# Grouping 1024 tokens in a fused attention and soft-MoE kernel, with the slot sums in the next group's burst of logits

## The chip, the cores and the metric

The kernel runs on one core of a Trainium2 chip. The time is device microseconds of one execution of the whole program; three runs of the kernel before took 1529.78, 1530.56 and 1531.02 us. A profiled execution is one further run, with every instruction's start and length recorded.

In the profile the engines are: PE, TensorE's matrix products; PEld, its weight loads; DVE, VectorE; ACT, ScalarE; POOL, GpSimd; SP, SyncE, which issues the DMAs here.

## What is computed

Two stages, all in f32. The first is an attention without softmax, for 8 batches of 2496 tokens, with keys and queries both z (64 wide) and values v (256 wide):

```
scores = z @ z.T / 2496
x      = u * (max(scores, 0)**2 @ v)            # 8 x 2496 x 256
```

The second is a soft mixture of experts on the 19968 tokens x, with 32 slots (8 experts of 4 slots):

```
logits     = x @ phi                            # 19968 x 32
d          = exp(logits - logits.max(0))        # over all tokens
slot_input = (d / d.sum(0)).T @ x               # 32 x 256: the slot sums
slot_out   = relu(slot_input @ w1) @ w2         # per expert
c          = exp(logits - logits.max(1)); c /= c.sum(1)     # combine weights
out        = c @ slot_out
```

## The kernel before, in words

The attention goes chunk by chunk: a chunk is up to 512 queries of one batch (512, 512, 512, 512, 448; the last batch is cut so that it ends with two chunks of 256). Each chunk has 5 steps over the keys, each step 4 key tiles of 128, and each step two halves. `scores` (line 175) makes two score tiles on PE (tile `sc`), ScalarE applies relu and square (tile `r`), and VectorE splits the result into a rounded part `ph` and its remainder `pl`. `attend` (line 216) then multiplies these with the values, split in the same way, into the tile `acc`: 24 products in a half step, on two row halves of 64 at a time, so that two products run side by side. The main loop (line 465) lets `scores` run one step ahead: in front of each half of `attend` it calls `between`, which runs the functions left in the list `begin`, then at most one piece of `work`, then `pair`, which makes the scores of the next step. Lists `middle` and `behind` hold work that other engines do between relu and square, and behind the remainders.

PE, ScalarE and VectorE are wrapped in `InOrder` (line 38): their instructions keep the order in which the code issues them. All of them therefore have line 46 in the profile, the line of the wrapper, and are told apart by their tiles. DMAs on SP have no such wrapper.

When a chunk is complete, `finish_chunk` (line 276) multiplies `acc` with `u` into the tile `xg` of a group of 512 tokens, 39 groups in all. A complete group puts four calls of the generator `group` (line 291) into `work`, and they run in the half steps of the next chunk, from the second step on:

1. logits (tile `lg`): 16 products of the 32-slot phi with 128 tokens each, laid out so that token quarter t stands on rows 32 t to 32 t + 31 of the result. Each row half (h) of the 128 feature rows gives its own partial result in its own half `ps[:, h]` of the tile, 512 columns each; VectorE adds the two into L, takes the maximum and updates the running maximum. ScalarE's exponentials E wait in `middle`.
2. transposes of the tokens (tile `tr`), which ScalarE copies to `xt`. Columns 256 and 257 of `xt` hold ones.
3. transposes of L and E (tile `le`). From L's transpose the combine weights `cw` follow, through `begin` and `middle`.
4. slot sums (tile `sl`): 8 products of E's transpose with `xt`, 258 columns wide; column 256 is thereby the sum of the exponentials. VectorE rescales `slot_acc` by the change of the maximum, adds half 0, and then half 1.

All four tiles share one buffer of the pool `ms_ps`. The accumulators `acc` (2), the score tiles (2) and this tile fill the PSUM memory. Behind the attention part come the transposes of `cw` (`turn`, line 392), the experts and the output; line numbers from 500 on belong to them. There ScalarE and VectorE each copy one half of the columns of a tile `sT_ps` (lines 528 and 529).

Of the kernel before, what the change touches and what calls it, by code (L numbers as in the profile page):

```python
# [20 lines left out]
NW = 32  # L21
KT = 20
QC = 512
NQ = 5
NG = N // 512
SMALL, LARGE = [(0, 2), (37, 2), (34, 3)], [(g, 4) for g in range(2, 34, 4)]
ROT = S - QC * (NQ - 1)
NP = KT // 4
# [21 lines left out]
def attn_soft_moe_kernel(ctx, tc, uT, v, zz, phi, ww, outT):  # L50
    nc = tc.nc

    pe, act, dve = (InOrder(tc, x) for x in (nc.tensor, nc.scalar, nc.vector))

    cpool = ctx.enter_context(tc.tile_pool(name="cpool", bufs=1))
# [4 lines left out]
    ms_ps = att_ps.enter_context(tc.tile_pool(name="ms_ps", bufs=1, space=PSUM))  # L60
# [3 lines left out]
    xpool = moe.enter_context(tc.tile_pool(name="xpool", bufs=1))  # L64
    HALF = [slice(0, 64), slice(64, 128)]
# [49 lines left out]
    xt = [xpool.tile([P, 4, 258], F32, name=f"xt{i}") for i in range(2)]  # L115
    slot_acc = [cpool.tile([P, 258], F32, name=f"slot_acc{i}") for i in range(2)]
    runmax = [cpool.tile([P, 1], F32, name=f"runmax{i}") for i in range(2)]
    cw = cpool.tile([P, NG, P], F32, name="cw")

    def constants():  # L120
        make_identity(nc, ident)


        nc.gpsimd.memset(esel, 0.0)
        nc.gpsimd.memset(rsel, 0.0)
        for h in range(4):
            rows = slice(h * NS, (h + 1) * NS)
            nc.gpsimd.tensor_copy(
                esel[rows, :, 0:SE], ident[rows, rows].rearrange("k (e s) -> k e s", s=SE)
            )  # L130
# [8 lines left out]
        for t in xt:  # L139
            nc.gpsimd.memset(t[:, :, 256:258], 1.0)  # L140
# [135 lines left out]
    def finish_chunk(b, ch, acc):  # L276
        _, _, n, t0 = ch
        ut = ut_.pop(t0)
        s = 0
        while s < n:  # L280
            g, o = divmod(t0 + s, 512)
            w = min(n - s, 512 - o)
            if g not in xg_:
                xg_[g] = wk.tile([P, 2, 512], F32, tag="xg", name=f"xg_{g}")
            dve.tensor_mul(xg_[g][:, :, o : o + w], acc[:, :, s : s + w], ut[:, :, s : s + w])
# [5 lines left out]
    def group(g):  # L291

        x = xg_.pop(g)

        ps = ms_ps.tile([P, 2, 512], F32, tag="ms", name=f"lg_{g}")
# [7 lines left out]
        L = wk.tile([P, P], F32, tag="L", name=f"L_{g}")  # L305
        E = wk.tile([P, P], F32, tag="E", name=f"E_{g}")
        m = wk.tile([P, 4], F32, tag="m", name=f"m_{g}")
        mnew, mold = runmax[g % 2], runmax[(g + 1) % 2]
        dve.tensor_copy(L, ps[:, 0, 0:P])
        dve.tensor_add(L, L, ps[:, 1, 0:P])  # L310
        if g == 0:
            dve.reduce_max(mnew, L, axis=AX.X)
        else:
            dve.reduce_max(m[:, 0:1], L, axis=AX.X)
            dve.tensor_max(mnew, m[:, 0:1], mold)
            dve.tensor_sub(m[:, 2:3], mold, mnew)
        dve.tensor_scalar_mul(m[:, 1:2], mnew, -1.0)

        def exps():
            act.activation(E, L, AF.Exp, bias=m[:, 1:2])  # L320
            if g:
                act.activation(m[:, 3:4], m[:, 2:3], AF.Exp)

        middle.append(exps)
        yield

        ps = ms_ps.tile([P, 2, 512], F32, tag="ms", name=f"tr_{g}")
        for t in range(4):
            for c in range(2):
                for h, rows in enumerate(HALF):  # L330
                    pe.transpose(
                        ps[:, h, t * P + c * 64 : t * P + (c + 1) * 64],
                        x[rows, c, t * P : (t + 1) * P], ident[rows, rows],
                    )
        xs = xt[g % 2]
        act.copy(
            xs[:, :, 0:D].rearrange("p t (h q) -> p h t q", h=2),
            ps.rearrange("p h (t q) -> p h t q", q=P),
        )
        yield  # L340

        ps = ms_ps.tile([P, 2, 512], F32, tag="ms", name=f"le_{g}")
        for k, m_ in enumerate((L, E)):
            for h, rows in enumerate(HALF):
                pe.transpose(ps[:, h, k * 64 : (k + 1) * 64], m_[rows], ident[rows, rows])
        le = wk.tile([P, 2, P], F32, tag="le", name=f"le_{g}")
        act.copy(le, ps[:, :, 0:P])
        rm = wk.tile([P, 2, 4], F32, tag="rm", name=f"rm_{g}")
        lt = le[:, :, 0:64].rearrange("p h (b s) -> p h b s", s=NS)
        cg = cw[:, g].rearrange("p (h b s) -> p h b s", b=2, s=NS)  # L350

        def rows_of(i):
            return rm[:, i].rearrange("p (h b) -> p h b", b=2)

        def spread(i):
            return rows_of(i).unsqueeze(3).to_broadcast([P, 2, 2, NS])

        def combine():
            dve.tensor_reduce(rows_of(0), lt, axis=AX.X, op=ALU.max)
            dve.tensor_sub(cg, lt, spread(0))  # L360
            middle.append(combine_exp)

        def combine_exp():
            act.activation(cw[:, g], cw[:, g], AF.Exp)
            begin.append(combine_sum)

        def combine_sum():
            dve.tensor_reduce(rows_of(1), cg, axis=AX.X, op=ALU.add)
            dve.tensor_scalar_add(rm[:, 1], rm[:, 1], 1e-9)
            dve.reciprocal(rm[:, 1], rm[:, 1])  # L370
            dve.tensor_mul(cg, cg, spread(1))

        begin.append(combine)
        yield

        ps = ms_ps.tile([P, 2, 512], F32, tag="ms", name=f"sl_{g}")
        for t in range(4):
            e = le[:, t // 2, 64 + t % 2 * NS : 64 + (t % 2 + 1) * NS]
            for h, rows in enumerate(HALF):
                pe.matmul(  # L380
                    ps[t * NS : (t + 1) * NS, h, 0:258], e[rows], xs[rows, t], start=True, stop=True
                )
        snew, sold = slot_acc[g % 2], slot_acc[(g + 1) % 2]
        if g == 0:
            dve.tensor_copy(snew, ps[:, 0, 0:258])
        else:
            dve.scalar_tensor_tensor(
                snew, sold, m[:, 3:4], ps[:, 0, 0:258], op0=ALU.mult, op1=ALU.add
            )
        dve.tensor_add(snew, snew, ps[:, 1, 0:258])  # L390

    def turn(g0, ng):

# [103 lines left out]


    ep = ctx.enter_context(tc.tile_pool(name="ep", bufs=1))
    sfin = slot_acc[(NG - 1) % 2]  # L500

    mfin = runmax[(NG - 1) % 2]
# [27 lines left out]
    for eg in range(2):  # L532
        nc.tensor.matmul(
            pn[:, eg : eg + 1], fsel[:, eg * P : (eg + 1) * P],
            sfin[:, 256:257], start=True, stop=True,
        )
    rs = ep.tile([P, 2], F32, name="rs")
    nc.vector.tensor_scalar_add(rs, pn[:, 0:2], 1e-9)
# [165 lines left out]
```

## Time and profile before

| | before |
|---|---|
| median of 3 runs | 1530.56 us |
| the profiled execution's own time | 1529.76 us |
| its span, first to last instruction | 1528.0 us |
| mean granted TensorE clock | 0.985 |
| PE busy | 1499.4 us, 15332 products |
| VectorE busy | 1158.0 us |
| ScalarE busy | 1033.0 us |

Busy time of an engine is the union of its instructions' times. Products overlap on PE, and their ends are modelled, so that what a burst costs is read from the starts of the work behind it. In the chain of waits each row is a start, a length and the work that stood on the path to the end. The page's group rows give an operation, its tiles (out<-in), shapes and count, then busy time and mean ns of one, then the engine's idle time ahead of it and who ended it. In timeline rows a start, a length and a merged run of equal instructions are followed in brackets by the idle time ahead of them and its releaser.

### The profile page before, as it was taken

The page shows a single profiled execution, that of the slowest core. Times are in us where ns is not written, and L with a number is a line of the kernel's source. Part 1 is how long each engine was busy: PE and PEld are TensorE (multiplying, and loading weights), DVE is VectorE, ACT ScalarE, POOL GpSimd, SP SyncE. Part 2 cuts the span into 40 slices and gives each one's busy share as a digit, 9 for nine tenths or more (in the row PEclk, how much of TensorE's full clock was granted, in tenths as well). Part 3 has the DMA queues.
Part 4 walks back from the last instruction along what each step waited for, and adds up shares of the span by engine and source line. Part 5 has one row for each costly group of instructions (what it writes and reads, how often), then busy time and mean ns, then how long its engine had stood idle before and what let it go on. Part 6 is the DMA issues. An engine that isn't in the chain of part 4 may idle for free.

```text
span 1528.0 us, 38187 instructions
## 1 busy us (share of the span) xinstructions
PE 1499.4 (98%) x15332; PEld 1203.0 (79%) x15332; DVE 1158.0 (76%) x2466; ACT 1033.0 (68%) x2043; POOL 3.2 (0%) x23
## 2 busy tenths in 40 slices
PE   8999999999999999999999999999999999999985
PEld 6877887788777887778777787778877788778853
DVE  6878866877778876788778886788777887676753
ACT  7777766767667666777668676676667776666543
POOL 0000000000000000000000000000000000000000
PEclk9999999999999999999999999999999999999995
DMA  4111200111001210112001110011101131000659
GB/s 146 29 29 55 57 24 27 41 52 54 15 22 48 57 36 15 29 55 59 20 16 50 54 57 15 22 48 50 43 15 29 49 122 45 26 9 8 242 236 392
DMA packets 36657, 91.62 MB, mean 60 GB/s; under 512 B 3712, under 2 KB 6272, under 8 KB 34432
## 3 DMA queue, kind: packets, MB, share of 16 engines
q1 hardware_dynamic: 36480, 89.18, 18.2%
q8 instruction: 121, 1.98, 0.5%
q14 instruction: 56, 0.46, 0.1%
HBM read 68.71 MB, written 20.45 MB: 58 GB/s over the span
## 4 chain that ended last, share of the span: by engine, by line
PE 96%; DMA 2%; DVE 1%; ACT 0%; issue 0%; DVEq 0%; SPq 0%; ACTq 0%
PE acc L46 70%; PE sc L46 19%; DMA outT<-ot 2%; PE lg L46 2%; PE sl L46 2%; PE tr L46 1%; PE h L552 0%; PE po L574 0%; DVE ot L634 0%; PE le L46 0%; PE pf L628 0%; DMA zr<-in_zz 0%; PE cT L396 0%; DVE cw L397 0%; PE so L605 0%
## 5 line engine op out<-in xcount | busy, mean ns | idle before, releaser
L46 PE MATMUL acc<-ph,v 64*128 64x512 f32 (+2 forms) x6384 | 996.7, 383 | 0.0
L46 PEld LDWEIGHTS acc<-ph,v 64*128 64x128 f32 x6384 | 617.5, 185 | 120.2 <-issue 0.2
L46 ACT ACTIVATE r<-sc 128x512 f32<-128x512 f32 (+2 forms) x820 | 428.4, 575 | 388.3 <-PE sc L46 386.8
L46 PE MATMUL acc<-pl,v 64*128 64x512 f32 (+2 forms) x3190 | 639.4, 382 | 0.0
L46 DVE TENSOR_TENSOR pl<-r,ph 128x512 fp32r<-128x512 f32 (+4 forms) x819 | 546.0, 667 | 66.8 <-PE acc L46 1.4
L46 DVE CAST ph<-r 128x512 fp32r<-128x512 f32 (+2 forms) x820 | 336.1, 410 | 240.6 <-ACT r L46 237.6
L46 ACT ACTIVATE r<-r 128x512 f32<-128x512 f32 (+2 forms) x820 | 455.0, 610 | 0.0
L46 PEld LDWEIGHTS acc<-pl,v 64*128 64x128 f32 x3190 | 318.8, 185 | 57.5
L46 PE MATMUL sc<-z,z 64*128 64x512 f32 (+2 forms) x1920 | 275.8, 391 | 0.0
L46 PEld LDWEIGHTS sc<-z,z 64*128 64x128 f32 x1920 | 170.9, 185 | 46.0 <-issue 18.2
L46 PE MATMUL sc<-z 64*128 64x512 f32 (+2 forms) x480 | 69.9, 393 | 0.0
L46 DVE TENSOR_TENSOR z<-zr,z 64x512 fp32r<-64x512 f32 x80 | 54.9, 686 | 2.5
L46 DVE TENSOR_TENSOR v<-vr,v 128x512 fp32r<-128x512 f32 x80 | 54.9, 686 | 1.6 <-ACT v L46 1.4
L46 ACT CAST v<-vr 128x512 fp32r<-128x512 f32 x80 | 49.4, 618 | 8.9 <-PE sc L46 8.9
L46 PEld LDWEIGHTS sc<-z 64*128 64x128 f32 x480 | 43.1, 185 | 10.3 <-issue 4.9
L46 DVE TENSOR_TENSOR xg<-acc,ut 128x512 f32<-128x512 f32 (+7 forms) x71 | 49.7, 736 | 1.8 <-PE acc L46 1.8
L46 ACT CAST z<-zr 64x512 fp32r<-64x512 f32 x80 | 49.6, 620 | 1.9
L46 ACT COPY xt<-tr 128x1024 f32<-128x1024 f32 x39 | 39.5, 1013 | 11.7 <-PE tr L46 11.7
L634 DVE COPY ot<-pf 128x1024 f32<-128x1024 f32 (+2 forms) x22 | 24.3, 1102 | 21.2 <-DMA outT<-ot 16.3
L628 PE MATMUL pf<-cp,soh 32*128 32x512 f32 (+2 forms) x176 | 27.2, 587 | 10.7 <-ACT ot L634 8.4
L634 ACT COPY ot<-pf 128x1024 f32<-128x1024 f32 (+2 forms) x22 | 20.2, 917 | 25.2 <-DMA outT<-ot 19.8
L628 PEld LDWEIGHTS pf<-cp,soh 32*128 32x128 f32 x176 | 14.1, 258 | 22.9 <-ACT ot L634 16.5
(86 smaller groups left out, 481.3 us busy)
## 6 DMA issues: line engine op xcount, KB each, us to landing
vr<-in_v SPq DMA_DIRECT2D x80, 256.0 KB, 2.7
w<-in_w SPq DMA_DIRECT2D x32, 512.0 KB, 5.8
outT<-ot SPq DMA_DIRECT2D x16, 1024.0 KB, 8.4
ut<-in_uT SPq DMA_DIRECT2D x31, 512.0 KB, 3.7
zr<-in_zz SPq DMA_DIRECT2D x40, 256.0 KB, 2.7
ut<-in_uT SPq DMA_DIRECT2D x8, 448.0 KB, 3.4
outT<-ot SPq DMA_DIRECT2D x4, 512.0 KB, 5.4
outT<-ot SPq DMA_DIRECT2D x2, 768.0 KB, 5.7
```

What stands on the lines that cost most here:

```text
L46: return lambda *a, **k: self.tc.keep_in_program_order(f(*a, **k))
L628: nc.tensor.matmul(pf[t // 2][:, t % 2, :ng], a[rows, c], parts[g0][rows, k, :ng], start=(m == 0), stop=(m == 2), tile_position=(t * NS, 0),)
L634: x = (nc.vector.tensor_copy if tp else nc.scalar.copy)(o, pf[tp][:, :, :ng])
```

## The change

A group is now 1024 tokens, a pair of the former groups: 19 pairs and a last one with 512 tokens, numbered q = 0 to 19. The generator gets six calls: logits; nothing; transposes of the first 512 tokens; of the second; transposes of L and E; and for the last two groups only, slot sums in a call of their own. For q = 0 to 17 the slot sums are kept in `late` and issued in the next group's logits call, ahead of the logits and into the same tile: the sums take columns 0 to 255 of each half, the logits columns 256 to 511 (256 for the last, of 128). VectorE's reads of the sums are issued between the two.

The ones columns of `xt` go, so slot-sum products have 256 columns, and the sums of exponentials come out of ScalarE's exponential by its accumulator (`accum_out`), from where VectorE adds them in an instruction of their own. The instructions on L, E, cw and their copies take both 512-token halves at once. `xt` is one tile for both halves; L and E have one buffer in place of two; `ut`, the loaded u of a chunk, has one buffer in place of two; `xg` is twice as large.

```diff
@@ finish_chunk
-            g, o = divmod(t0 + s, 512)
-            w = min(n - s, 512 - o)
...
-            if o + w == 512:
-                it = group(g)
-                work.extend([lambda it=it: next(it, None)] * 4)
+            q, o = divmod(t0 + s, 1024)
+            w = min(n - s, 1024 - o)
...
+            if o + w == 1024 or t0 + s + w == N:
+                it = groups(q)
+                work.extend([lambda it=it: next(it, None)] * 6)
@@ group -> groups
+        nj = min(2, NG - 2 * q)
+        n = nj * P
+        ps = ms_ps.tile([P, 2, 512], F32, tag="ms", name=f"lg_{q}")
+        sums = late.pop() if late else None
+        if sums:
+            sums(ps)
+        xj = x.rearrange("p c (j t k) -> p c t j k", j=2, k=P)
         for c in range(2):
             for t in range(4):
                 for h, rows in enumerate(HALF):
                     pe.matmul(
-                        ps[t * NS : (t + 1) * NS, h, 0:P], phi_sb[rows, c],
-                        x[rows, c, t * P : (t + 1) * P], start=(c == 0), stop=(c == 1),
+                        ps[t * NS : (t + 1) * NS, h, D : D + n], phi_sb[rows, c],
+                        xj[rows, c, t, :nj], start=(c == 0), stop=(c == 1),
                     )
...
+        dve.tensor_copy(L[:, :n], ps[:, 0, D : D + n])
+        dve.tensor_add(L[:, :n], L[:, :n], ps[:, 1, D : D + n])
...
-            act.activation(E, L, AF.Exp, bias=m[:, 1:2])
+            act.activation(E[:, :n], L[:, :n], AF.Exp, bias=m[:, 1:2], accum_out=m[:, 4:5])
...
+        def slot_sums(ps):
+            for j in range(nj):
+                for t in range(4):
+                    e = le[:, 1, j, t * NS : (t + 1) * NS]
+                    for h, rows in enumerate(HALF):
+                        pe.matmul(
+                            ps[t * NS : (t + 1) * NS, h, 0:D], e[rows], xt[rows, j, t],
+                            start=(j == 0), stop=(j == nj - 1),
+                        )
+            snew, sold = slot_acc[q % 2], slot_acc[(q + 1) % 2]
+            if q == 0:
+                dve.tensor_copy(snew[:, 0:D], ps[:, 0, 0:D])
+                dve.tensor_copy(snew[:, D : D + 1], m[:, 4:5])
+            else:
+                dve.scalar_tensor_tensor(
+                    snew[:, 0:D], sold[:, 0:D], m[:, 3:4], ps[:, 0, 0:D], op0=ALU.mult, op1=ALU.add
+                )
+                dve.scalar_tensor_tensor(
+                    snew[:, D : D + 1], sold[:, D : D + 1], m[:, 3:4], m[:, 4:5],
+                    op0=ALU.mult, op1=ALU.add,
+                )
+            dve.tensor_add(snew[:, 0:D], snew[:, 0:D], ps[:, 1, 0:D])
+
+        if q < NQG - 2:
+            late.append(slot_sums)
+            return
         yield
+        slot_sums(ms_ps.tile([P, 2, 512], F32, tag="ms", name=f"sl_{q}"))
@@ load_u
-        ut = wa.tile([P, 2, QC], F32, tag="ut", name=f"ut_{t0}")
+        ut = wa.tile([P, 2, QC], F32, tag="ut", name=f"ut_{t0}", bufs=1)
```

More of the change, by code (lines that the diff above doesn't have):

```diff
@@ L113, in attn_soft_moe_kernel @@
     one = cpool.tile([1, 1], F32, name="one")
-    xt = [xpool.tile([P, 4, 258], F32, name=f"xt{i}") for i in range(2)]
-    slot_acc = [cpool.tile([P, 258], F32, name=f"slot_acc{i}") for i in range(2)]
+    xt = xpool.tile([P, 2, 4, D], F32, name="xt")
+    slot_acc = [cpool.tile([P, D + 1], F32, name=f"slot_acc{i}") for i in range(2)]
     runmax = [cpool.tile([P, 1], F32, name=f"runmax{i}") for i in range(2)]
@@ L280, in finish_chunk, with groups @@
         while s < n:
-            g, o = divmod(t0 + s, 512)
-            w = min(n - s, 512 - o)
-            if g not in xg_:
-                xg_[g] = wk.tile([P, 2, 512], F32, tag="xg", name=f"xg_{g}")
-            dve.tensor_mul(xg_[g][:, :, o : o + w], acc[:, :, s : s + w], ut[:, :, s : s + w])
-            if o + w == 512:
-                it = group(g)
-                work.extend([lambda it=it: next(it, None)] * 4)
-            s += w
-    def group(g):
-        x = xg_.pop(g)
-        ps = ms_ps.tile([P, 2, 512], F32, tag="ms", name=f"lg_{g}")
+            q, o = divmod(t0 + s, 1024)
+            w = min(n - s, 1024 - o)
+            if q not in xg_:
+                xg_[q] = wk.tile([P, 2, 1024], F32, tag="xg", name=f"xg_{q}")
+            dve.tensor_mul(xg_[q][:, :, o : o + w], acc[:, :, s : s + w], ut[:, :, s : s + w])
+            if o + w == 1024 or t0 + s + w == N:
+                it = groups(q)
+                work.extend([lambda it=it: next(it, None)] * 6)
+            s += w
+    late = []
+    def groups(q):
+        x = xg_.pop(q)
+        nj = min(2, NG - 2 * q)
[5 more added lines that the diff above has]
+        xj = x.rearrange("p c (j t k) -> p c t j k", j=2, k=P)
         for c in range(2):
@@ L301, in group @@
                     pe.matmul(
-                        ps[t * NS : (t + 1) * NS, h, 0:P], phi_sb[rows, c],
-                        x[rows, c, t * P : (t + 1) * P], start=(c == 0), stop=(c == 1),
-                    )
[L305 to L312, printed above, removed]
+                        ps[t * NS : (t + 1) * NS, h, D : D + n], phi_sb[rows, c],
+                        xj[rows, c, t, :nj], start=(c == 0), stop=(c == 1),
+                    )
+        L = wk.tile([P, 2 * P], F32, tag="L", name=f"L_{q}", bufs=1)
+        E = wk.tile([P, 2 * P], F32, tag="E", name=f"E_{q}", bufs=1)
+        m = wk.tile([P, 5], F32, tag="m", name=f"m_{q}")
+        mnew, mold = runmax[q % 2], runmax[(q + 1) % 2]
+        dve.tensor_copy(L[:, :n], ps[:, 0, D : D + n])
+        dve.tensor_add(L[:, :n], L[:, :n], ps[:, 1, D : D + n])
+        if q == 0:
+            dve.reduce_max(mnew, L[:, :n], axis=AX.X)
         else:
-            dve.reduce_max(m[:, 0:1], L, axis=AX.X)
+            dve.reduce_max(m[:, 0:1], L[:, :n], axis=AX.X)
             dve.tensor_max(mnew, m[:, 0:1], mold)
@@ L325, in group @@
         yield
-        ps = ms_ps.tile([P, 2, 512], F32, tag="ms", name=f"tr_{g}")
-        for t in range(4):
-            for c in range(2):
+        yield
+        for j in range(nj):
+            ps = ms_ps.tile([P, 2, 512], F32, tag="ms", name=f"tr_{q}_{j}")
+            for t in range(4):
+                for c in range(2):
+                    for h, rows in enumerate(HALF):
+                        pe.transpose(
+                            ps[:, h, t * P + c * 64 : t * P + (c + 1) * 64],
+                            x[rows, c, (4 * j + t) * P : (4 * j + t + 1) * P], ident[rows, rows],
+                        )
+            act.copy(
+                xt[:, j].rearrange("p t (h k) -> p h t k", h=2),
+                ps.rearrange("p h (t k) -> p h t k", k=P),
+            )
+            yield
@@ L330, in group @@
+        ps = ms_ps.tile([P, 2, 512], F32, tag="ms", name=f"le_{q}")
+        for k, m_ in enumerate((L, E)):
+            for j in range(nj):
                 for h, rows in enumerate(HALF):
+                    o = (2 * k + j) * 64
                     pe.transpose(
-                        ps[:, h, t * P + c * 64 : t * P + (c + 1) * 64],
-                        x[rows, c, t * P : (t + 1) * P], ident[rows, rows],
-                    )
[L335 to L350, printed above, removed]
@@ L352, in rows_of @@
-        def rows_of(i):
-            return rm[:, i].rearrange("p (h b) -> p h b", b=2)
+                        ps[:, h, o : o + 64], m_[rows, j * P : (j + 1) * P], ident[rows, rows]
+                    )
+        le = wk.tile([P, 2, 2, P], F32, tag="le", name=f"le_{q}")
+        lx, px = le.rearrange("p k j (h b) -> p h (k j) b", h=2), ps.rearrange("p h (k b) -> p h k b", b=64)
+        if nj == 2:
+            act.copy(lx, px[:, :, 0:4])
+        else:
+            act.copy(lx[:, :, 0::2], px[:, :, 0:4:2])
@@ L355, in spread @@
+        rm = wk.tile([P, 2, 8], F32, tag="rm", name=f"rm_{q}")
+        lt = le[:, 0, :nj].rearrange("p j (t s) -> p (j t) s", s=NS)
+        cg = cw[:, 2 * q : 2 * q + nj]
+        cs = cg.rearrange("p j (t s) -> p (j t) s", s=NS)
         def spread(i):
-            return rows_of(i).unsqueeze(3).to_broadcast([P, 2, 2, NS])
+            return rm[:, i, : 4 * nj].unsqueeze(2).to_broadcast([P, 4 * nj, NS])
         def combine():
-            dve.tensor_reduce(rows_of(0), lt, axis=AX.X, op=ALU.max)
@@ L370, in combine_sum @@
-            dve.reciprocal(rm[:, 1], rm[:, 1])
-            dve.tensor_mul(cg, cg, spread(1))
+            dve.tensor_reduce(rm[:, 1, : 4 * nj], cs, axis=AX.X, op=ALU.add)
+            dve.tensor_scalar_add(rm[:, 1, : 4 * nj], rm[:, 1, : 4 * nj], 1e-9)
+            dve.reciprocal(rm[:, 1, : 4 * nj], rm[:, 1, : 4 * nj])
+            dve.tensor_mul(cs, cs, spread(1))
         begin.append(combine)
-        yield
[L376 to L390, printed above, removed]
+        def slot_sums(ps):
+            for j in range(nj):
+                for t in range(4):
+                    e = le[:, 1, j, t * NS : (t + 1) * NS]
+                    for h, rows in enumerate(HALF):
+                        pe.matmul(
[3 more added lines that the diff above has]
+            snew, sold = slot_acc[q % 2], slot_acc[(q + 1) % 2]
+            if q == 0:
+                dve.tensor_copy(snew[:, 0:D], ps[:, 0, 0:D])
+                dve.tensor_copy(snew[:, D : D + 1], m[:, 4:5])
+            else:
+                dve.scalar_tensor_tensor(
+                    snew[:, 0:D], sold[:, 0:D], m[:, 3:4], ps[:, 0, 0:D], op0=ALU.mult, op1=ALU.add
+                )
+                dve.scalar_tensor_tensor(
+                    snew[:, D : D + 1], sold[:, D : D + 1], m[:, 3:4], m[:, 4:5],
+                    op0=ALU.mult, op1=ALU.add,
+                )
+            dve.tensor_add(snew[:, 0:D], snew[:, 0:D], ps[:, 1, 0:D])
@@ L499, in attn_soft_moe_kernel @@
     ep = ctx.enter_context(tc.tile_pool(name="ep", bufs=1))
-    sfin = slot_acc[(NG - 1) % 2]
-    mfin = runmax[(NG - 1) % 2]
+    sfin = slot_acc[(NQG - 1) % 2]
+    mfin = runmax[(NQG - 1) % 2]
     pm = ms_ps.tile([P, 512], F32, tag="ms", name="pm")
@@ L534, in attn_soft_moe_kernel @@
             pn[:, eg : eg + 1], fsel[:, eg * P : (eg + 1) * P],
-            sfin[:, 256:257], start=True, stop=True,
+            sfin[:, D : D + 1], start=True, stop=True,
         )
```

12 lines of the change are left out of this document (5 added, 7 removed).

## The prediction

> **What bounds the kernel now.** I read the page first: the table of engines, the slices and the chain that ended last.
>
> ```profile
> span 1528.0 us, 38187 instructions
> ...
> PE 1499.4 (98%) x15332; PEld 1203.0 (79%) x15332; DVE 1158.0 (76%) x2466; ACT 1033.0 (68%) x2043; POOL 3.2 (0%) x23
> ...
> PE   8999999999999999999999999999999999999985
> ...
> PE 96%; DMA 2%; DVE 1%; ACT 0%; issue 0%; DVEq 0%; SPq 0%; ACTq 0%
> ```
>
> TensorE (PE) is busy in every slice from the second on to the end of the attention part, and the chain runs through it for 96% of the span. There a microsecond taken out of PE's queue is a microsecond of the kernel, and one for which PE stands still is lost. VectorE (DVE, 76%) and ScalarE (ACT, 68%) count only through waits that they put on PE.
>
> Next I read the price of the group work on PE, in the chain over one group's four bursts (columns: start, length, what).
>
> ```profile
> 440.79 2.80 PE acc L46 x24
> ...
> 444.28 2.80 PE acc L46 x24
> 447.08 0.60 PE lg L46 x32
> ...
> 448.57 2.80 PE acc L46 x24
> ...
> 452.61 2.81 PE acc L46 x24
> 455.43 0.12 PE le L46 x4
> ...
> 456.30 2.80 PE acc L46 x24
> 459.10 0.60 PE sl L46 x16
> ...
> 460.59 2.81 PE acc L46 x24
> ...
> 464.11 2.80 PE acc L46 x24
> ```
>
> A half step is 24 attention products (acc) and 6 score products. From one acc start to the next it takes 444.28 - 440.79 = 3.49 us without a burst and 464.11 - 460.59 = 3.52 behind the last one: 3.50. With the logits (lg) it takes 448.57 - 444.28 = 4.29, so they cost 0.79; with the token transposes (tr) 4.04, so 0.54; with those of L and E (le) 3.69, so 0.19; with the slot sums (sl) 4.29, so 0.79. A group costs 2.31 us of PE, two groups 4.62. Of lg's and sl's 0.79, 0.60 is the burst and 0.19 the way in and out of it.
>
> **The change, part by part.** First what PE saves. The columns that pass stay about the same; an entry and exit and the start of a burst fall away.
>
> ```profile
> L46 PE MATMUL lg<-xg,phi_sb 64*32 64x128 f32 x1248 | 26.4, 275 | 0.0
> L46 PE MATMUL sl<-xt,le 64*32 64x258 f32 x624 | 26.0, 390 | 0.0
> ```
> ```profile
> 699.66 2.47 PE acc L46 x24
> ```
>
> The group rows differ by 390 - 275 = 115 ns for 130 columns: 0.885 ns a column. The acc row is of a chunk with 448 columns: 2.47 us for 2.80, and its products go in 12 pairs, so 0.33 / 12 / 64 = 0.43 ns a column. A product of plain f32 thus costs about two such passes, 0.84 to 0.89; I take 0.84, the price in a full pipe. Eight products stand side by side (four token quarters by two row halves), so lg has 32 / 8 = 4 rounds of 128 columns, and sl has 2 of 258. The new burst has 4 rounds of 256 for the logits of 1024 tokens, and 4 of 256 for the sums of the pair before. From lg's 0.79 on, that is 4 x 128 x 0.84 = 0.43 for the wider logits and 4 x 256 x 0.84 = 0.86 for the sums: 2.08 (2.15 at 0.885), for 4 x 0.79 = 3.16. Two tr bursts stay, 1.08. The le burst has 8 transposes for 4: 0.19 + 0.12 = 0.31, for 0.38. So a pair takes 3.47 in place of 4.62, and saves 1.15. Eighteen bursts are merged (pairs 1 to 18, each with the sums of the pair before): 20.7 us. Pair 0's logits and pair 18's sums stand alone at 0.79 + 0.43 for 1.58, which with the le bursts saves 0.8 more; group 38 is done alone, as now. In all 21.5 us (20.2 at 0.885). The empty second step costs nothing, since two chunks have 16 free places for the six steps.
>
> Then the wait that it adds. In the merged burst the slot-sum products fill columns 0 to 255 of both halves of one tile. Behind them the code has VectorE read them: slot_acc takes half 0, then its count column is made, then half 1 is added. Behind those stand the logits, which write columns 256 to 511 of the same halves. The columns differ; must the logits wait all the same? The trace has two engines at one half of such a tile only at the end, where ScalarE and VectorE copy different columns of sT_ps (lines 528 and 529).
>
> ```profile
> 1452.47 0.34 DVE L519 TENSOR_SCALAR fsel<-esel,fac 128x256 f32<-128x256 f32 x1
> ...
> 1452.87 1.13 PE L524 MATMUL sT_ps<-fsel,slot_acc 128*128 128x256 f32 x4 [0.91 <-DVE fsel L519]
> ...
> 1454.09 0.37 ACT L528 COPY sT<-sT_ps 128x256 f32<-128x256 f32 x1 [1.96 <-PE sT_ps L524]
> 1454.37 0.16 DVE L538 TENSOR_SCALAR rs<-pn 128x2 f32<-128x2 f32 x1 [1.56 <-PE pn L533]
> ...
> 1454.65 0.40 DVE L529 COPY sT<-sT_ps 128x256 f32<-128x256 f32 x1
> ```
>
> The sums ended at 1454.00 and VectorE was idle, yet it took line 538, which stands later in the code, and copied its own columns only at 1454.65, after ScalarE's copy had ended at 1454.46. That is how a program looks in which two engines are kept apart by half, and not by column. I take it that the logits wait for VectorE's last read.
>
> The Trainium skill, "PSUM — Partial Sum Buffer", section "PSUM bank collisions raise a hardware error", speaks against this change in the same sense: two engines at one bank and the same 32 partitions at once are an error of the run, even at disjoint columns, so accesses must be guarded by bank. By that rule every merged burst holds such a wait; the sT rows agree, though they show two readers and not PE against a reader.
>
> When does VectorE come to these reads? It is behind PE. Three logits bursts show it, one of each kind:
>
> ```profile
> 447.01 0.67 PE L46 MATMUL lg<-xg,phi_sb 64*32 64x128 f32 x32
> ...
> 448.15 0.28 DVE L46 COPY L<-lg 128x128 f32<-128x128 f32 x1
> 448.47 0.29 DVE L46 TENSOR_TENSOR L<-L,lg 128x128 f32<-128x128 f32 x1
> ...
> 450.62 0.43 DVE L46 CAST ph<-r 128x512 fp32r<-128x512 f32 x1 [1.09 <-ACT r L46]
> ```
> ```profile
> 483.63 0.67 PE L46 MATMUL lg<-xg,phi_sb 64*32 64x128 f32 x32
> ...
> 485.70 0.29 DVE L46 COPY L<-lg 128x128 f32<-128x128 f32 x1
> ```
> ```profile
> 698.19 0.67 PE L46 MATMUL lg<-xg,phi_sb 64*32 64x128 f32 x32
> ...
> 699.90 0.28 DVE L46 COPY L<-lg 128x128 f32<-128x128 f32 x1
> ```
>
> The weights' remainders (ph, pl) of the half step before keep VectorE until 448.15 - 447.01 = 1.14 us after the burst's start; 2.07 where a split of z stands ahead as well, 1.71 where a split of v does. The merged bursts stand where the logits of groups 3, 5, ... 37 stand now: I read off 11 of the first kind, 3 with z (third chunk of a batch) and 4 with v (fifth chunk). The reads themselves:
>
> ```profile
> L46 DVE SCALAR_TENSOR_TENSOR slot_acc<-slot_acc,m,sl 128x258 f32<-128x258 f32 x38 | 18.2, 478 | 0.3 <-PE sl L46 0.3
> L46 DVE TENSOR_TENSOR slot_acc<-slot_acc,sl 128x258 f32<-128x258 f32 x39 | 16.5, 424 | 1.3
> L46 DVE TENSOR_TENSOR runmax<-m,runmax 128x1 f32<-128x1 f32 x38 | 6.1, 159 | 1.3
> ```
>
> 0.48 for half 0; some 0.08 for the count column, priced as its nearest row (0.16) half hidden under its neighbours; 0.04 between dependent instructions (448.15 + 0.28 to 448.47); 0.42 for half 1; and 0.06 until PE takes it up (fsel ends at 1452.81, PE starts at 1452.87): 1.08 us. PE itself is through with the sums' columns after 0.89. So PE stands still for 1.14 + 1.08 - 0.89 = 1.33 us in the plain case, 1.90 with v, 2.26 with z. If the count column is wholly hidden each is 0.08 less; if it and each hand-over cost in full, 0.15 more. The sum is 11 x 1.33 + 4 x 1.90 + 3 x 2.26 = 29.0 us, with 27.6 and 31.7 at the ends. Nothing gives it back: PE has no other work in its queue order, and the later chain is PE's own.
>
> Everything else is off PE's path. VectorE and ScalarE do one wide instruction for two narrow ones, which is less work; cover gone, they would matter only where weights come late (rival D). The accumulator of the exponentials and the two copies in following half steps go by these rows:
>
> ```profile
> L46 ACT ACTIVATE E<-L,m 128x128 f32<-128x128 f32 x39 | 15.7, 403 | 13.8 <-DVE m L46 13.8
> L46 ACT COPY xt<-tr 128x1024 f32<-128x1024 f32 x39 | 39.5, 1013 | 11.7 <-PE tr L46 11.7
> ```
> ```profile
> ut<-in_uT SPq DMA_DIRECT2D x31, 512.0 KB, 3.7
> ```
>
> No row shows an accumulator; between nothing and a second 0.40 us it stays under ScalarE's idle time, so I take nothing. A half step with a copy of 1.01 lasts 4.04 on PE, so that is covered too. In the last two chunks, of 256 columns, it lasts only 2.31:
>
> ```profile
> 1408.23 1.41 PE acc L46 x24
> ...
> 1410.54 1.41 PE acc L46 x24
> ```
>
> There pair 18 puts the copies, the wide burst and its sums where group 37 alone stood, and I allow 0.7 us (0 to 2). With one buffer of ut the load of a chunk waits for the product of the chunk before, a few us into the chunk; 3.7 us of load stand against the ten half steps of 3.5 until its use, so nothing, and the v and z loads queued behind it on SP are wanted several half steps later. Were that cover gone it would be 3.7 us a chunk.
>
> The sum: -21.5 + 29.0 + 0.7 = +8.2. The profiled execution's own time is 1529.76, of which 1528.0 is span; so 1538.0. The median shown, 1530.56, lies 0.8 above it; the same sum there gives 1538.8. I forecast 1538.
>
> **The rivals.**
>
> A, the forecast: the wait costs more than the merging saves. 1538.
>
> B, no wait: the logits follow the sums at once because only columns are compared. PE saves 21.5 us and the time is 1530.6 - 21 = 1510. For it: the halves' columns are disjoint, and a reader against PE is not in the trace. Against it: the sT copies, which were kept apart with disjoint columns. The point from which it decides: a mean stall below 21.5 / 18 = 1.2 us a burst turns the sign.
>
> C, the wait is there but about as dear as the saving: VectorE's reads overlap better and are hidden under the sums' tail (1.14 + 0.9 - 0.95 = 1.1 plain, 25 us in all), while the saving comes to 22 or 23. For it: VectorE's instructions overlap by some 0.08 where they don't depend. Time: 1529 to 1534.
>
> D, the wait and a second one: the running maximum comes later, ScalarE's exponentials wait for it with its squares queued behind them, so ph is late and PE waits for weights too. Now ph follows 3.6 us after a logits burst (450.62 - 447.01); the attention products that need it come two half steps, 7 us, after. For it: the burst and its reads put some 2.5 us on the chain. Against: 1 us is left. Overrun by 0.5 to 1 us in half the bursts gives 5 to 9 us more: 1543 to 1547.
>
> **How the numbers follow.** A 0.58, B 0.12, C 0.17, D 0.13. This kernel's measurements tell 0.2% (3 us) from no change. B is faster; C is within; A and D are slower, of A a little (0.01) counted to each other side: faster 0.13, same 0.18, slower 0.69. The range takes in C, A and most of D, 1529 to 1546, and leaves out B and a bit of D. Forecast A's own range, by the ends of the saving (20.2 to 22.5) and of the stall (27.6 to 31.7), is 1535 to 1543.
>
> **What would show it.** In the profile after: PE busy falls by about 22 us while the span grows; the view of waits has PE's logits waiting for DVE's slot_acc, 18 times, 25 to 32 us together, the longest about 2.3. In the chain a merged burst shows about 0.9 us of sums, a gap of 1.3 to 2.3, and about 1.0 of logits; DVE's addition to slot_acc ends just ahead of the logits. A half step without a burst stays at 3.50, tr at 0.54 more. Wrong would be: logits following the sums with no gap (then B, and the sign flips), a merged burst well over 2.1 us without its gap (the column price), or PE's attention products waiting for ph (D).

## The result, and the profile after

The changed kernel takes 1549.08 us, median of 4 runs (1548.91 to 1552.72), against 1530.28 (1529.78 to 1531.02) for the kernel before: a ratio of 1.0128, with a 95% interval of 1.0111 to 1.0146. It is slower, as forecast, but by 18.8 us and not by 8; the forecast was 1538 and its range ended at 1546. The profiled execution took 1548.91.

First the page of the kernel after: the span, the table of engines, TensorE's slices and the chain that ended last.

```profile
span 1546.8 us, 36940 instructions
...
PE 1490.8 (96%) x14724; PEld 1225.9 (79%) x14724; DVE 1114.2 (72%) x2205; ACT 1025.5 (66%) x1987; POOL 3.1 (0%) x21
...
PE   8999999999999999999999999999999999999985
...
PE 86%; DVE 7%; issue 2%; DMA 2%; ACT 1%; DVEq 0%; SPq 0%; ACTq 0%
```

TensorE (PE) still looks full in every slice, and no slice tells where 19 us went. The chain does: PE's share fell from 96% to 86%, VectorE's (DVE) rose from 1% to 7%, and ScalarE (ACT) has its first per cent, although both do less work than before. What they hold up stands in the view of waits of the kernel after (who waits, for whom: us in all, how often, the longest).

```profile
PEld lg L47 <- DVE slot_acc L47: 33.1, 18, 2.4
PE lg L47 <- DVE slot_acc L47: 24.4, 18, 2.0
...
ACT cw L47 <- DVE cw L47: 15.3, 18, 1.7
PEld acc L47 <- DVE pl L47: 10.7, 23, 0.5
...
PEld acc L47 <- DVE ph L47: 2.8, 14, 0.3
```

There are two families. The first two rows are the forecast wait: the logits (products and their weight loads) stand 18 times for VectorE's reads of slot_acc (the two rows overlap in time and do not add up; the ends of products are modelled, so the price of a stop is read from starts below). The last three are not in the forecast's sum. ScalarE waits 15.3 us with the exponential of the combine weights (cw); in the kernel before the same wait came to 4.2 us. And PE's attention products wait for their weights pl and ph.

One merged burst in the timeline of the kernel after (start, length, engine, what):

```profile
411.69 1.09 PE L47 MATMUL lg<-xt,le 64*32 64x256 f32 x32
...
412.22 0.69 DVE L47 TENSOR_TENSOR pl<-r,ph 128x512 fp32r<-128x512 f32 x1
...
412.89 0.48 DVE L47 SCALAR_TENSOR_TENSOR slot_acc<-slot_acc,m,lg 128x256 f32<-128x256 f32 x1
...
413.42 0.41 DVE L47 TENSOR_TENSOR slot_acc<-slot_acc,lg 128x256 f32<-128x256 f32 x1
...
413.89 1.10 PE L47 MATMUL lg<-xg,phi_sb 64*32 64x256 f32 x32 [1.10 <-DVE slot_acc L47]
```

The sums start at 411.69, VectorE comes to its reads when pl is done, ends them at 413.83, and the logits start at 413.89: 2.20 us behind the start of the burst, where the prediction worked out 2.22 (1.14 + 1.08).

To see where all of the 18.8 us lie I took the starts of the score products (sc) of every half step from both traces. There are 410 in each (41 chunks of 10 half steps), and the n-th of one is the n-th of the other, so the lengths can be compared one by one:

| half steps | forecast | measured |
|---|---|---|
| one with a merged burst, plain (4.18 to 6.81 us) | +2.62 | +2.63 |
| one with a split of v ahead, with a split of z ahead | +3.19, +3.55 | +3.13, +3.49 |
| the 18 merged bursts together | +52.2 | +51.9 |
| all with group work, and the one behind it | +8.2 | +8.6 |
| all others, with what lies ahead of the first start and behind the last | 0 | +10.2 |

The forecast's whole sum came out to 0.4 us. Part of that is luck: 1.5 us of the 8.6 stand in one half step (from 1214.83 on) in which PE's products ran slow, which the last section takes up, and without them the row would be 7.1. The other 10.2 us stand in half steps in which the changed kernel does no group work on PE, and nearly all of them at one place. Behind every chunk in which a group's logits run and that is the third or fifth of its batch (the last batch excepted), the half step with the next chunk's first attention products is long: eight of them, by 1.01 to 1.11 us each, 8.4 in all. Another 1.4 us stand in the two half steps ahead of each of these, and 0.87 in the same place of the last chunk; a half step at the very start is 0.6 shorter. One such place, first in the timeline of PE in the kernel before, then in the kernel after:

```profile
652.44 0.86 PE L46 MATMUL sc<-z,z 64*128 64x512 f32 x6
655.49 0.86 PE L46 MATMUL sc<-z,z 64*128 64x512 f32 x6
658.99 0.85 PE L46 MATMUL sc<-z,z 64*128 64x512 f32 x6
```
```profile
658.10 0.96 PE L47 MATMUL sc<-z,z 64*128 64x512 f32 x5
...
661.22 0.39 PE L47 MATMUL sc<-z,z 64*128 64x512 f32 x1
...
665.75 0.84 PE L47 MATMUL sc<-z,z 64*128 64x512 f32 x6
```

The half step that took 658.99 - 655.49 = 3.50 us now takes 665.75 - 661.22 = 4.53. What the other engines do meanwhile, in the timeline of the kernel after:

```profile
652.48 1.41 DVE L47 TENSOR_TENSOR z<-zr,z 64x512 fp32r<-64x512 f32 x2
...
653.81 0.40 DVE L47 TENSOR_REDUCE rm<-le 128x8 f32<-128x256 f32 x1
...
654.25 0.42 DVE L47 TENSOR_TENSOR cw<-le,rm 128x256 f32<-128x256 f32 x1
...
654.71 0.42 ACT L47 ACTIVATE cw<-cw 128x256 f32<-128x256 f32 x1 [1.67 <-DVE cw L47]
655.03 1.14 ACT L47 ACTIVATE r<-r 128x512 f32<-128x512 f32 x2
...
655.68 0.43 DVE L47 CAST ph<-r 128x512 fp32r<-128x512 f32 x1 [1.01 <-ACT r L47]
...
658.07 0.42 DVE L47 TENSOR_REDUCE rm<-cw 128x8 f32<-128x256 f32 x1
...
659.31 0.42 DVE L47 CAST ph<-r 128x512 fp32r<-128x512 f32 x1
...
664.27 0.19 PEld L47 LDWEIGHTS acc<-pl,v 64*128 64x128 f32 x2 [0.50 <-DVE pl L47]
...
665.27 1.22 DVE L47 TENSOR_TENSOR xg<-acc,ut 128x1024 f32<-128x1024 f32 x1
...
665.41 0.19 PEld L47 LDWEIGHTS acc<-pl,v 64*128 64x128 f32 x2 [0.50 <-DVE pl L47]
```

And the same stretch, the end of the same chunk, in the kernel before:

```profile
647.65 1.41 DVE L46 TENSOR_TENSOR z<-zr,z 64x512 fp32r<-64x512 f32 x2
...
648.98 0.41 DVE L46 CAST ph<-r 128x512 fp32r<-128x512 f32 x1
...
651.71 0.43 DVE L46 CAST ph<-r 128x512 fp32r<-128x512 f32 x1 [0.39 <-ACT r L46]
...
657.69 1.28 DVE L46 TENSOR_TENSOR xg<-acc,ut 128x384 f32<-128x384 f32 x2
```

Before, VectorE goes from the split of z straight to the next ph (647.65 to 648.98), and from there to the chunk's last product xg in 657.69 - 647.65 = 10.04 us. After, it takes 665.27 - 652.48 = 12.79, which is 2.75 more. The rows add up to it: behind the split stand the first pieces of the combine weights (653.81 to 654.67, some 0.8 us of VectorE's time). ScalarE has their exponential in its queue, in order and ahead of the squares r, waits 1.67 us for its input, and so the squares come late and VectorE waits 1.01 for them, where it waited 0.39 before. Then the third piece, the sum, takes 658.07 to 659.31, another 1.24. That is 0.8 + 1.0 - 0.4 + 1.24 = 2.7 us. Of these PE loses 1.02, in the two waits of 0.50 us for pl. In the kernel before, the combine pieces of a group came two half steps earlier (from 640.63 on), right behind the burst of slot sums, which made its half step on PE 4.27 us long.

### The profile page after: what moved, and what is told of

Same layout as the page of the kernel before. It is cut to its first block, busy times and chain, and to the rows that moved or that the text cites. A ratio compares the mean times of both kernels' runs of the same rounds, so it can differ in the third digit from the quotient of the medians.

```text
span 1546.8 us, 36940 instructions
## 1 busy us (share of the span) xinstructions
PE 1490.8 (96%) x14724; PEld 1225.9 (79%) x14724; DVE 1114.2 (72%) x2205; ACT 1025.5 (66%) x1987; POOL 3.1 (0%) x21
## 4 chain that ended last, share of the span: by engine, by line
PE 86%; DVE 7%; issue 2%; DMA 2%; ACT 1%; DVEq 0%; SPq 0%; ACTq 0%
PE acc L47 64%; PE sc L47 17%; DMA outT<-ot 2%; DVE ph L47 2%; PE lg L47 1%; DVE pl L47 1%; DVE z L47 1%; PE tr L47 1%; DVE slot_acc L47 1%; ACT r L47 1%; PE h L580 0%; PE po L602 0%; DVE ot L662 0%; DVE v L47 0%; PE le L47 0%
## 5 line engine op out<-in xcount | busy, mean ns | idle before, releaser
L47 PE MATMUL acc<-ph,v 64*128 64x512 f32 (+2 forms) x6384 | 1010.2, 384 | 0.0
L47 PEld LDWEIGHTS acc<-ph,v 64*128 64x128 f32 x6384 | 639.2, 185 | 108.5 <-DVE ph L47 2.8
L47 PE MATMUL acc<-pl,v 64*128 64x512 f32 (+2 forms) x3190 | 666.4, 384 | 1.3
L47 PEld LDWEIGHTS acc<-pl,v 64*128 64x128 f32 x3190 | 336.3, 185 | 62.4 <-DVE pl L47 10.7
L47 PEld LDWEIGHTS sc<-z,z 64*128 64x128 f32 x1920 | 182.3, 185 | 35.5 <-issue 6.6
L47 DVE TENSOR_TENSOR xg<-acc,ut 128x1024 f32<-128x1024 f32 (+7 forms) x56 | 48.7, 892 | 1.8 <-PE acc L47 1.8
L47 PE MATMUL lg<-xg,phi_sb 64*32 64x256 f32 (+1 forms) x640 | 21.9, 377 | 24.4 <-DVE slot_acc L47 24.4
L47 PEld LDWEIGHTS lg<-xg,phi_sb 64*32 64x32 f32 x640 | 10.0, 106 | 35.9 <-DVE slot_acc L47 33.1
```

The source lines that it names most:

```text
L47: return lambda *a, **k: self.tc.keep_in_program_order(f(*a, **k))
```

## The experiments

Two theories stood after the comparison, one for each family of waits. The first (W): the stall is the wait between PE and VectorE at one half of a tile, as predicted. The second (H1): the 10 us come from the combine pieces, which now stand at the chunk's end. Against H1 stood two rivals: that the single buffer of ut costs the time (H2), and that the stop of PE in the burst throws everything behind it out of step (H3), so that no stall would mean no late half step. Later runs tell two readings of H1 apart: that VectorE's pieces do it, the sum above all, or that ScalarE's exponential does it, which holds up the squares behind it.

### The combine pieces put off by six half steps

```
-        begin.append(combine)
+        def put_off(k):
+            if k:
+                begin.append(lambda: put_off(k - 1))
+            else:
+                combine()
+
+        begin.append(lambda: put_off(6 if q < NQG - 2 else 0))
```

> The changed kernel (1549.1 us) with one edit: the combine weights' three pieces on VectorE and ScalarE are put off by six half steps, into the next chunk, where no group work stands. Theory H1, that some 11 us of the loss come from these pieces standing on VectorE just ahead of the weights (ph, pl) of the next chunk's first step, behind splits of z and v: the attention products there no longer wait, and the time falls by 9 to 11 us to 1538 to 1540, about the 1538 of the forecast. Theory H2, that the single buffer of u (late loads on SP) holds these half steps up: no change, 1549. Theory H3, that the 1.3 to 2.3 us stop in the merged burst throws the later work out of step: no change, 1549.

Measured: 1543.5 us (1540.82 to 1544.24), ratio 1.0082 (1.0067 to 1.0097). All eight long half steps are back at 3.50, which with the two ahead of each gives 9.8 us back. But 9 to 11 in all were expected, and 5.6 came. The pieces arrive in the middle of other chunks, and where a split of z stands ahead of them they do the same thing again: 2.1 us in six half steps of three chunks. The chain of this kernel over the first of them:

```profile
452.26 0.68 DVE z L47
452.94 0.34 DVE rm L47
...
453.31 0.44 DVE cw L47
...
453.77 0.42 ACT cw L47
454.19 0.53 ACT r L47
...
454.74 0.44 DVE ph L47
...
457.52 0.50 PE acc L47 x2
```

Split, maximum, difference, exponential, square, ph, and at the end PE: the whole mechanism in seven rows. The place of the pieces decides, not the chunk's end as such, and this place was a poor one. The rest of what is missing has another reason: in two further places of this trace, 3.1 us in all, PE's clock is lower for a while (last section), and the changed kernel's trace has only one such place, of 1.5 us.

### One buffer of ut in the kernel before

```
-        ut = wa.tile([P, 2, QC], F32, tag="ut", name=f"ut_{t0}")
+        ut = wa.tile([P, 2, QC], F32, tag="ut", name=f"ut_{t0}", bufs=1)
```

> The kernel before (1530.3 us) with one buffer for the loaded u in place of two, and nothing else. H1 and H3: no change, within 1 us of 1530.3, since the load has ten half steps. H2: the loads of z and v queue behind it and the half steps at the chunks' start get longer, by about 11 us, 1541.

Measured: 1529.86 us, ratio 0.9998 (0.9988 to 1.0007). The single buffer costs nothing in the kernel before. No run has two buffers in the changed kernel; but several runs below keep its single buffer and lose the long half steps, as the run above does. So H2 falls.

### The logits first, then the sums, then all reads

```
-        if sums:
-            sums(ps)
 ...the 32 logits products...
+        add_sums = sums(ps) if sums else None
 ...VectorE: copy L, add, maximum...
+        if add_sums:
+            add_sums()
```

`sums(ps)` issues only the 32 products here (32 as the trace counts: each of the 16 plain f32 products in the code makes two MATMUL rows), and hands back the three instructions of VectorE that read them. So no instruction of VectorE stands between the two bursts.

> The changed kernel (1549.1 us) with the merged burst turned round: the logits' products first, the slot sums' products behind them, and all of VectorE's reads behind both, so that PE has nothing in the burst that waits for VectorE. If the wait for VectorE's reads is what the burst costs (theory W, the forecast's 29 us): half steps with a burst go from 6.81 to about 5.48 us where nothing else stands, the time falls by 27 to 30 us to 1519 to 1522. Rival B', that the burst is long because of its products themselves (wide columns, two kinds of operands): no change, 1549. H1: the late half steps at the chunks' start stay, some 10 us of them. H3: they go as well, and the time falls by 38 us to about 1511.

Measured: 1519.53 us (1519.08 to 1520.3), ratio 0.9929 (0.9915 to 0.9944), 29.5 below the changed kernel. The chain of this kernel over the merged burst that was shown above:

```profile
404.45 2.80 PE acc L47 x24
407.25 1.89 PE lg L47 x64
409.14 0.90 PE sc L47 x6
```

The 64 products go in one piece of 1.89 us, and a plain half step with a burst lasts 5.47 in place of 6.81. The prediction's terms give the same: 4.18 for the half step with the old logits, less their 0.79, plus 2.08 for the merged burst. So W is confirmed in its cause and its size: the 18 half steps with a merged burst are 28.7 us shorter together, for a forecast stall of 29.0. (The medians differ by 29.5; the changed kernel's slow half step of 1.5 us is gone too.) The view of waits of this kernel has no row of PE waiting for slot_acc any more, but these are as they were:

```profile
ACT cw L47 <- DVE cw L47: 15.3, 18, 1.7
...
PEld acc L47 <- DVE pl L47: 10.7, 23, 0.5
```

The eight long half steps stay too (9.8 us, with the two ahead of each). PE doesn't stop in the burst any more, and still the later work is late: H3 falls. One of the eight already spoke against it in the changed kernel: it stands behind the first group's logits, whose burst has no sums and no stop.

### The grouping alone, the sums on their own

```
-        if q < NQG - 2:
-            late.append(slot_sums)
-            return
         yield
```

> The changed kernel (1549.1 us) without the putting off: each group of 1024 tokens does its slot sums in its own sixth half step and in a tile of its own. This is the grouping alone. By the prices of the prediction a pair then takes 1.22 + 1.22 + 1.08 + 0.31 = 3.83 us of PE for 4.62, no wait is in a burst: 15 us less than before, 1515, and with H1's late half steps, to which VectorE's 1 us of reads is added at the end of the chunk, 11 to 18 us more: 1526 to 1533. H3: no late half steps, 1515.

Measured: 1517.13 us (1516.36 to 1517.64), ratio 0.9913 (0.9898 to 0.9928). That is far below what H1 had foreseen and near H3's figure, and for H3 it would have spoken, had the run before not shown the long half steps without a stall. In the trace the long half steps are gone (3.50 and 3.60), and the view of waits says what is different:

```profile
ACT cw L47 <- DVE cw L47: 1.8, 4, 0.4
...
PEld acc L47 <- DVE pl L47: 1.5, 6, 0.3
```

Here a burst of slot sums, 1.1 us more on PE, stands in the very half step in which the combine pieces run, and gives VectorE and ScalarE that time. H1 had been right on the mechanism, but its expectation had left out that the kernel puts this cover back. Against the run before, a half step with logits is 0.86 us shorter here and one with the sums 1.12 longer: taken by itself, and without the stall, the merging saves only 0.26 us a burst, some 5 us in all, and loses its cover, 8 to 10 us.

### The sum alone put off by three half steps

```
-            begin.append(combine_sum)
+            begin.append(lambda: put_off(3 if q < NQG - 2 else 0))
```

> The changed kernel (1549.1 us), with VectorE's last piece of the combine weights alone (sum, reciprocal, product: 1.2 us) put off by three half steps, to behind the chunk's product with u; the maximum and ScalarE's exponential stay where they are. Theory H1v, that it is VectorE's queue ahead of the weights that is late: the late half steps go as in the first run, nothing new is late, and the time falls by 10 to 11 us, to 1538 to 1539. Theory H1a, that ScalarE's exponential ahead of the squares is what makes them late: no change, 1549.

> Logits first (1519.5 us) and the sum put off by three half steps. H1v: the two are independent, 1519.5 - 10.5 = 1509, the time that the prediction gave for a merged burst without a wait (1510). H1a: 1519.5. If the 10 us are only moved to another half step: 1515 to 1519.

The second of the two has the turned burst as well. Measured: 1545.2 us (1544.82 to 1547.8), ratio 1.01 (1.0085 to 1.0115), and 1517.06 (1515.04 to 1518.09), ratio 0.9913 (0.9896 to 0.9929). Behind the fifth chunks the long half step is cured (-0.9 to -1.1 us each). Behind the third chunks it is only moved: -1.02 us there, and +0.90 two half steps later, where the sum now meets the next delay. 1538 to 1539 had been expected of the first, so the sum piece alone isn't the cause; ScalarE's wait of 15.3 us was untouched.

### No empty second step

In the turned burst's kernel:

```
-                work.extend([lambda it=it: next(it, None)] * 6)
+                work.extend([lambda it=it: next(it, None)] * 5)
...
         middle.append(exps)
         yield
-        yield
```

> Logits first (1519.5 us) with the empty second step left out, so that the transposes of L and E and the three pieces behind them come one half step sooner, and the last piece still ahead of the chunk's end. H1v: the late half steps get shorter by at least half, or go: 1509 to 1514. A theory that they are late through the chunk's own work (splits of z and v and the product with u), whatever stands ahead: no change, 1519.5.

Measured: 1515.5 us (1513.89 to 1517.31), ratio 0.9903 (0.9888 to 0.9918), 4.0 below the kernel with the turned burst alone and just above the expected 1509 to 1514. All that moves is when the transposes and the combine pieces come: one half step earlier. ScalarE's wait for cw falls from 15.3 to 5.6 us. All eight long half steps are at 3.50; of the 9.8 us, 3.0 stay in the half steps just ahead of them.

### The exponential one half step later

```
-            middle.append(combine_exp)
+            if q < NQG - 2:
+                begin.append(lambda: middle.append(combine_exp))
+            else:
+                middle.append(combine_exp)
```

> The changed kernel (1549.1 us) with ScalarE's exponential of the combine weights put off by one half step alone; so the sum behind it on VectorE also comes one half step later. Theory H4, that the chain of the late weights begins on ScalarE, whose queue stands behind this exponential while VectorE has still to make its input (15.3 us of waiting in 18 places, 4.2 before), so that squares, ph and pl are all late: the wait goes to under 4 us, the late half steps lose most of their 1.0 us, and the time falls by 7 to 10 us, to 1539 to 1542. Theory H1v, that VectorE's 1.2 us of sum is enough by itself: the sum only moves by one half step within the crowded stretch, 1546 to 1549.

Measured: 1544.74 us (1544.64 to 1547.57), ratio 1.0097 (1.008 to 1.0113): 4.3 less, where 7 to 10 were expected. ScalarE's wait is gone from the view of waits, and the long half steps shrink by only 0.3 us behind third chunks and 0.56 behind fifth ones (0.22 behind the first of these); with the two ahead of each, 4.5 of the 9.8 us come back. Two other places get longer, by 1.5 and 1.6 us, but there it is PE's clock that is lower, as in the first run (last section). So taking ScalarE's wait away, with the sum one half step later as well, gives back about half.

With the turned burst, and the sum put off as well (three half steps in all):

> Logits first (1519.5 us), the exponential put off by one half step and the sum by three in all. H4 and H1v together (both are needed): no late half step left in the stretch, 1508 to 1511. If VectorE has simply too much work in that stretch: the lateness moves on, 1513 to 1517, as when the sum alone was put off (1517.1).

Measured: 1512.16 us (1510.79 to 1513.36), ratio 0.9884 (0.9869 to 0.9898); 1508 to 1511 had been expected. It is 7.4 below the turned burst alone. All eight long half steps are at 3.50; in four of the chunks 0.62 us comes back two half steps later, behind a split of z and the sum. ScalarE's queue in this kernel, in the timeline:

```profile
640.61 1.09 ACT L47 ACTIVATE r<-sc 128x512 f32<-128x512 f32 x2 [1.39 <-PE sc L47]
641.58 0.42 ACT L47 ACTIVATE cw<-cw 128x256 f32<-128x256 f32 x1
```

The exponential finds its input there, and ScalarE's only wait is the ordinary one, for PE's scores.

### Turned burst, no empty step, exponential later

> Logits first without the empty step (1515.5 us), with the exponential put off by one half step. H4: what is left there of ScalarE's wait (5.6 us) goes, and 3 to 5 us with it: 1510 to 1512. If VectorE's amount of work is what is left: no change, 1515.

Measured: 1511.12 us (1510.65 to 1511.97), ratio 0.9878 (0.9863 to 0.9892), the fastest here, 19 us below the kernel before. The page of this kernel:

```profile
span 1508.5 us, 36987 instructions
...
PE 1478.9 (98%) x14724; PEld 1232.3 (82%) x14724; DVE 1114.8 (74%) x2205; ACT 1023.5 (68%) x1987; POOL 3.1 (0%) x21
```

In the view of waits PE's attention products wait for pl only 0.4 us in all, and nowhere for ph. With both families of waits gone the time is near what the prediction's rival B had worked out for the merged bursts without any wait: 1510.

## Why the prediction was wrong

**What bounds the kernel: right.** A microsecond on PE is one of the kernel, before as after.

**The saving of 21.5 us: right.** In the trace of the last experiment, which runs the same bursts without waits, the half steps with group work and those behind them are 20.5 us shorter than before, where the prediction has 21.5 less the 0.7 of the last chunks. (Its median is 18.6 below, 1511.12 for 1529.73 in the same session.) The price of 0.84 ns a column is a little under twice the 0.43 that the prediction read off, but the run bears it out: 5.47 - 4.18 = 1.29 us for 1536 columns more. PE busy, on the other hand, fell in the changed kernel by 8.6 us and not by 22, a sign of the prediction that did not come true. That row was a poor witness: in the last experiment it is 20.5 below before, so I read it that products slowed by late weights count as busy in it; no run tests that by itself.

**The wait in the burst, 29.0 us: right, place and price.** 18 waits, the longest 2.0 for the products and 2.4 for the weight loads; half steps longer by 51.9 for 52.2 us; and 28.7 us came back in them when the order of PE's and VectorE's instructions took the reason of the wait away. What the sT copies had let one suspect of two readers holds for PE against a reader: columns that do not overlap do not help in this program. So rival B (no wait) and rival C (a wait as dear as the saving) are out. (One label in the prediction is off: the three bursts with a split of z ahead stand in the fourth chunk of a batch, not the third. Their price isn't touched by it.)

**"Everything else is off PE's path": the step that failed.** It costed at nothing the move of the transposes of L and E, and of the combine pieces behind them two half steps later. In front of it stood the same error in another form: "The empty second step costs nothing, since two chunks have 16 free places for the six steps." Places on PE were counted; what the empty step moves on VectorE and ScalarE was not. Without it the kernel with the turned burst is 4.0 us faster. In place of nothing the runs showed 10.2 us, and the accounts close: 1538.0 + 10.2 + 0.4 in the half steps of the forecast's own terms is 1548.6, for 1548.91 in the profiled execution. In the 0.4 a slow half step of 1.5, which nobody had forecast, makes up for terms that came out 1.1 below it.

**Why that step was thought safe.** VectorE has 24% and ScalarE 32% of idle time over the span, and they do less work than before. But the pieces are a chain that goes VectorE, ScalarE, VectorE, and both engines work in order. A piece that comes late to VectorE, behind a split of z, doesn't cost its 0.4 us on ScalarE but the whole time that ScalarE stands for it, with the squares of the next weights behind it. The prediction asked what stands ahead of VectorE's reads in the burst, and priced it well; of the combine pieces it did not ask that.

**Rival D was near, and at the wrong place.** It named ScalarE's queue with the squares held behind a late exponential, PE waiting for ph, and 1543 to 1547. It had the exponentials of the logits in mind, right behind the burst, and there the rows show the opposite: ScalarE's wait for the running maximum (E behind m) was 13.8 us before, and is 2.6 after, of which 1.9 stand in the last group. What was late were the exponentials of the combine weights, five half steps on. The sign that it gave came true all the same: products wait for ph (2.8 us), and more so for pl (10.7).

**The costs taken as nothing.** ut with one buffer: right, shown in the kernel before and borne out by the runs that keep it. The accumulator: no wait in the trace hangs on it; it was not tried by itself.

What stays open: how the 10.2 us divide between ScalarE's wait and VectorE's sum. Each put right by itself gave about 4 us (3.9 and 4.3), both together 7.4 of the 10, and since both feed the same delay of VectorE there may be no such division. Why four chunks keep 0.62 us when both are put off isn't settled either; that it is the sum behind the split of z is read from one of them only.

## What to carry to other kernels

When a step moves in a schedule, follow every instruction that it issues on every queue to its new neighbours: a chain that crosses two in-order engines can hold up a full third one, though all of them have idle time on average, and a cover (here a burst on PE in the same half step) goes with the work that is moved away. If two bursts share a half of a tile, issue both of them before the first read of either: that alone turned 19 us of loss into 11 of gain. And when the changed step comes out as priced while the total doesn't, compare all equal steps of the two traces one by one; the missing time stood in steps that the change doesn't touch.

## What the hardware showed beside this

The accumulator of the exponentials is an instruction of its own on ScalarE, and the addition of the count column costs VectorE more than its nearest row in the trace of before (0.159 us for the maximum of two columns). The group rows of the kernel after:

```profile
L47 ACT ACTIVATE E<-L,m 128x256 f32<-128x256 f32 x19 | 9.7, 510 | 1.2 <-DVE m L47 0.7
...
L47 DVE SCALAR_TENSOR_TENSOR slot_acc<-slot_acc,m 128x1 f32<-128x1 f32 x19 | 4.0, 212 | 0.0
L47 ACT ACTIVATION_READ_ACCUMULATOR E<-L,m 128x1 f32 x20 | 3.7, 187 | 0.0
```

Reading it out takes 187 ns, 20 times, inside the 0 to 0.40 us that were allowed; the column takes 212 ns, of which 0.13 us fall between the neighbours (413.29 to 413.42 in the burst shown).

The mean granted clock of PE was 0.985 in the profiled execution of both kernels, and the mean hides something. PE stops 18 times in the changed kernel, for 1.1 to 2.0 us. Behind one of the three longest stops, 1.96 us with a split of z ahead, the clock was halved for 3.41 us. The windows below give the busy time of PE, of its weight loads, of VectorE, ScalarE and GpSimd (with counts), then the granted clock, the DMA share and GB/s:

```profile
1211.57:1214.98 3.41, 1.45 (x50) 0.65 (x36) 2.07 (x6) 0.00 (x0) 0.00 (x0) 1.00 0.29 77
1214.98:1218.39 3.41, 3.41 (x18) 2.66 (x20) 1.65 (x6) 2.00 (x6) 0.00 (x0) 0.50 0.00 0
1218.39:1221.80 3.41, 3.41 (x32) 2.77 (x30) 2.75 (x5) 2.17 (x5) 0.00 (x0) 1.00 0.00 0
```

The half step at 1214.83 took 5.15 us, and the same place behind the other two of the three takes 3.61: 1.5 us more. The traces of the put-off combine pieces and of the exponential one half step later have two such stretches each (from 485.78 and 847.59, and from 487.46 and 849.27), all behind such a stop. The put-off sum's trace, with the same stops, has none, and no kernel without these stops has one in its attention part. So a stop could cost more than its own length here. What decides whether it does no run shows, and with one trace of each kernel the link itself is not tested.
